# A Fourier mixing layer with a gated feed-forward on one core: fourteen instead of ten row tiles in seven products, sums formed by DMA, new buffers in the last stage

## The chip, the cores and the metric

The kernel runs on one core of a Trainium2 chip. The metric is the device time of one execution in microseconds. All engines of the core work from their own queues in order: PE (matrix products), DVE and ACT (elementwise work), POOL (elementwise work, and the issue of DMAs whose descriptors it makes itself) and SP (the issue of the other DMAs).

## The reference, cut to what matters

```python
x  = A_x                                   # 1 x 2048 x 448
xn = layernorm(x)                          # over the last axis
a  = einsum("bsd,ed->bse", xn, dft_hid_re)
b  = einsum("bsd,ed->bse", xn, dft_hid_im)
s  = einsum("ts,bse->bte", dft_seq_re, a) - einsum("ts,bse->bte", dft_seq_im, b)
g  = silu((gelu(xn @ w_gate) * (xn @ w_up)) @ w_down)     # 448 -> 1792 -> 448
out = x + s * g
```

All inputs are float32. The kernel splits operands into a high part rounded to the matmul's type and a low rest, and forms a product from two or three matmuls of the parts.

## The kernel before

There are 16 row tiles of 128 tokens (`NK`), read as four chunks of four. The work runs through these stages.

- **Normalization, and the first group of the feed-forward** (to about 73 us).
- **Blocks.** The remaining six groups `gi` = 1 to 6 of the feed-forward each take two of the 14 column tiles. `strassen` handles one column tile `f` for one half `p` of the tokens; four calls per group (`bi` = 0 to 3) make 24 blocks in a row. A block has five banks of products (x1 to x5), four pieces of the down product that are sent in between (`dn`, `send`, `down_one`), and at one place in the middle `preps()`, which prepares the weights of a later block. `prep_s` is that: four sums of 128 columns (L237 to L240; on POOL in blocks 2, 3, 5, 7 and every second one to 19, counted from 0), then two copies on ACT (L241, L242) and two subtractions on DVE (L243, L244) which split the weights. They stand on ACT and DVE between the block's own reads of its banks.
- **Hidden stage.** For each of 16 row tiles `k`, `hid_mm` makes the transforms a and b (22 matmuls); `hid_out` then either splits them plainly (`hid_plain`, six tiles `KP`) or forms eight half rows and their sums and splits seven of these (`hid_seven`, ten tiles). After the first two tiles the eight last pieces of the down product are sent.
- **Last stage.** Output rows are made in pairs `j` = 0 to 7 of two tiles each. A row tile k of the sum over the sequence goes into both outputs of a pair, either in seven products for the pair (`seven`: 7 matmuls of 448 columns and 7 of 224) or plainly (`plain`: 12 matmuls of 448). Ten tiles go in seven products and six plainly. The work is cut into units: two sevens to a loaded piece, each piece with its coefficients `ct` and two further sums of them on DVE (`combine_c`); 13 units per pair. `gather` combines the seven results into both outputs, `give` adds the plain part, multiplies by g and adds x, all on DVE; SP stores.

Four of the ten tiles (`KX`) do not fit in the core's memory together: two pairs of them take turns in two buffers, stored once to `td` and loaded again in each pair. The sums of coefficients that need no data are formed in DRAM during the blocks: `sum_copy(j)` copies by SP, `sum_add(j)` adds by two DMAs on POOL (L629), in turns, one call per block, ahead of the block's `strassen`.

The order of the work is written out by hand: the recording order of the program is each engine's order.

Of the kernel before, what the change touches and what calls it, by code (L numbers as in the profile page):

```python
# [30 lines left out]
KR = (0, 2, 4, 6, 9, 12)  # L31
KX = ((5, 8), (11, 14))
KP = (1, 3, 7, 10, 13, 15)
F_AT = {0: 0, 2: 0, 4: 1, 5: 0, 6: 1, 8: 0, 9: 1, 11: 0, 12: 1, 14: 1}

WHERE = "BAC"
UNITS = 13
DRAIN = {12: 2, 2: 2}


def order(j):


    q = [(t, k) for t in range(2) for k in KP]
    q = [q[i : i + 4] for i in range(0, 12, 4)]
    first = [KX[(j + 1) % 2], q[0]]
    return first[:: 1 if j else -1] + [KR[0:2], KR[2:4], KR[4:6], KX[j % 2], q[1], q[2]]

NS = 5


def slot_of(j, n):

    seven = [isinstance(what, tuple) for what in order(j)]
    return (0 if seven[n] else NS) + sum(s == seven[n] for s in seven[:n]), seven[n]

# [3 lines left out]
def fnet_geglu(ctx: ExitStack, tc: tile.TileContext, x, ct, et, wgu, wd, out):  # L62
# [20 lines left out]
    ps_mm = ctx.enter_context(tc.tile_pool(name="ps_mm", bufs=4, space=bass.MemoryType.PSUM))  # L83
    ps_tp = ctx.enter_context(tc.tile_pool(name="ps_tp", bufs=2, space=bass.MemoryType.PSUM))
    ps_o = ctx.enter_context(tc.tile_pool(name="ps_o", bufs=1, space=bass.MemoryType.PSUM))
# [6 lines left out]
    a_w = [sb.tile([P, 2560], FR, name=f"w{i}", tag=f"w{i}") for i in range(3)]  # L92
    a_d = [sb.tile([P, 1792], FR, name=f"wd{i}", tag=f"d{i}") for i in range(2)]
    a_r = sb.tile([P, 2 * 1536], F32, name="raw")
    a_t = sb.tile([P, 8 * 512], F32, name="tmp", tag="tmp")
# [16 lines left out]
    turns = [0]  # L112

    def o_tile(name, which=None):

        turns[0] += 1
        tag = which or "AB"[turns[0] % 2]
        return ps_o.tile([P, 512], F32, name=name, tag=tag)
# [44 lines left out]
    def turn_mm(c, k):  # L163
        pt = ps_tp.tile([P, 4, P], F32, name=f"pt{c}_{k}", tag="tp")
# [115 lines left out]
    def gu_ps(f, c):  # L280
        names = [f"gu{f}_{c}_{g}" for g in range(2)]
        if (f, c) == (0, 1):
            return [o_tile(n) for n in names]
        return [ps_mm.tile([P, 512], F32, name=n, tag="mm") for n in names]


    hs_of = {}

    def hs_tile(name, dt=FR):
        return sb.tile([P, 2, 512], dt, name=name, tag="hs", bufs=6)  # L290

    def new_hs(f, c):
        hs_of[f, c] = hs_tile(f"hs{f}_{c}")
        return hs_of[f, c]
# [3 lines left out]
    def act(f, c, pg):  # L298
        acts[0] += 1
        gt = tmp(acts[0] % 2)  # L300
# [17 lines left out]
    def down_one(gi, c, wdn, kk):  # L318
        if gi > 0 and kk >= 2:
            po = ps_tp.tile([P, 512], F32, name=f"po{gi}_{c}_{kk}", tag="tp")  # L320
        else:
            po = o_tile(f"po{gi}_{c}_{kk}")
# [36 lines left out]
    def strassen(f, p, w, late, dn, preps):  # L359
# [7 lines left out]
        def bank(i):  # L367
            return ps_mm.tile([P, 512], F32, name=f"x{i}_{f}_{p}", tag="mm")
# [19 lines left out]
        dn[1]()  # L388
        preps()
# [28 lines left out]
    with tc.manual_schedule():  # L418
# [11 lines left out]
        junk = hs_tile("junk")[:, 0]  # L430
# [124 lines left out]
        xf[2] = hs_tile("xf2", F32)  # L555
# [23 lines left out]
        for c in (2, 3):  # L579
# [6 lines left out]
            if c == 2:  # L586
                xf[3] = hs_tile("xf3", F32)
# [30 lines left out]

        sums = [dram.tile([P, NS, 512], F32, name=f"sums{j}") for j in range(NK // 2)]

        def sum_copy(j):
            src = ct[j, :NS].rearrange("n p c -> p n c")
            for q in range(2):
                nc.sync.dma_start(sums[j][:, :, 256 * q : 256 * (q + 1)], src[:, :, :256])

        def sum_add(j):
            src = ct[j, :NS].rearrange("n p c -> p n c")
            for n in (slice(0, 2), slice(2, NS)):
                nc.gpsimd.dma_start(sums[j][:, n], src[:, n, 256:768], accum_op=ALU.add)  # L629
# [13 lines left out]
        for gi in range(1, len(GROUPS)):  # L643
# [39 lines left out]
            def e_split(b):  # L683

                r = n_raw["e", b]
                if b == 3:
                    e_at[b] = []
                    for i in range(2):
                        w = a_w[slots[2 if i == 0 else 0]]
                        h, q = w[:, 1792 : 1792 + D], r[:, i * D : (i + 1) * D]  # L690
# [4 lines left out]
                if b == 1:  # L695
                    v = a_d[(gi + 1) % 2]
                else:
                    v = a_w[slots[2 if b == 0 else 0]][:, :1792]
# [3 lines left out]
            for bi, (i, p, prep) in enumerate(  # L702
# [33 lines left out]
        a_u = [sb.tile([P, 4096], FR, name=f"ts{p}", tag=f"u{p}") for p in range(2)]  # L736
# [3 lines left out]
        TS, ab = {}, {}  # L740
        fs = [a_r[:, : 4 * D], None]

        def hid_mm(k):
# [3 lines left out]
            for r in range(2):  # L747
                p = ps_mm.tile([P, 512], F32, name=f"ab{k}_{r}", tag="mm")
# [8 lines left out]
        def hid_plain(k, ps):  # L757
            spots = PLAIN[k]()
# [8 lines left out]
        def hid_seven(k, ps):  # L767


            f = fs[F_AT[k]].rearrange("p (i d) -> p i d", d=HD)  # L770
# [4 lines left out]
            nc.vector.tensor_sub(f[:, 4], f[:, 7], f[:, 0])  # L775
            nc.vector.tensor_sub(f[:, 3], f[:, 6], f[:, 7])
            nc.vector.tensor_sub(f[:, 5], f[:, 6], f[:, 4])
            nc.vector.tensor_sub(f[:, 1], f[:, 2], f[:, 5])
            t = SEVEN[k]()
            v = t.rearrange("p (i w d) -> p i w d", i=7, w=2)  # L780
            split(v[:, :, 0], v[:, :, 1], f[:, :7])
            TS[k] = t
            if k in td and k < NK - 2:
                nc.sync.dma_start(td[k], t.bitcast(F32))


        new = {}

        def place(name):

            if name not in new:
                if name[0] == "u":
                    new[name] = a_u[int(name[1])]
                elif name[0] == "x":
                    new[name] = a_x[int(name[1])]
                elif name == "t":
                    new[name] = sb.tile([P, 4096], FR, name="ts_t", tag="tmp")
                else:
                    new[name] = sb.tile([P, 8 * D], FR, name=f"ts_{name}", tag=name)
            return new[name]  # L800

        def seven_at(name):
            return lambda: place(name)[:, : 7 * D]

        def rest_of(*names):
            return lambda: [place(n)[:, 7 * D : 9 * D] for n in names]

        def in_hs(k):
            return lambda: [
                hs_tile(f"ab{k}_{r}").rearrange("p a b -> p (a b)")[:, : 2 * D] for r in range(2)  # L810
            ]

        SEVEN = dict(zip(KR, map(seven_at, ("u0", "u1", "t", "x0", "x1", "x2"))))
        SEVEN.update({k: seven_at(f"g{i}") for ks in KX for i, k in enumerate(ks)})
        spots = (rest_of("u0", "u1"), in_hs(1), in_hs(2), rest_of("t", "x0"), in_hs(3))
        PLAIN = dict(zip(KP, spots + (rest_of("x1", "x2"),)))

        def hid_out(k, ps):
            (hid_seven if k in SEVEN else hid_plain)(k, ps)


        pieces = [(j, n) for j in range(NK // 2) for n in range(8)]
        ring, bufs, c_raw = [], {}, {}

        def where(i):
            return WHERE[i % 3]

        waiting = {b: [i for i in range(len(pieces)) if where(i) == b] for b in "ABC"}

        def load_c(b):  # L830

            if waiting[b]:
                i = waiting[b].pop(0)
                j, n = pieces[i]
                c_raw[i] = bufs[b]
                s, seven = slot_of(j, n)
                if seven:
                    o = 512 if b == "B" else 0
                    nc.sync.dma_start(bufs[b][:, o : o + 768], ct[j, s][:, 256:])
                    nc.sync.dma_start(bufs[b][:, o + 768 : o + 1280], sums[j][:, s])  # L840
                else:
                    o = 768 if b == "B" else 0
                    nc.sync.dma_start(bufs[b][:, o : o + 1024], ct[j, s])

        def combine_c(i):


            v = c_raw[i].rearrange("p (i d) -> p i d", i=7)
            r, o = (2, 0) if where(i) == "B" else (0, 5)
            nc.vector.tensor_add(v[:, o], v[:, r + 4], v[:, r])  # L850
# [256 lines left out]
```

## Time and profile before

| what | value |
|---|---|
| median of 3 runs | 789.08 us (788.94 to 789.13) |
| profiled execution, its own time | 788.96 us |
| span of the profile | 787.2 us |
| PE busy | 780.8 us, 99% |
| DVE, ACT, POOL busy | 560.5, 297.9, 45.5 us |
| mean granted clock of PE | 0.999 |
| DMA moved | 123.81 MB |

The span runs from the first to the last instruction; the profiled execution's own time is 1.8 us longer. In rows of the order of time the first number is the start from the span's beginning, the second the duration, and what stands in square brackets is the idle time of the engine before the row and what ended it; "issue" means that nothing the profile shows was waited for. In rows of groups the numbers after the bar are busy time and the mean duration of one in ns, then idle time before them. In rows of DMA issues the last number is the median time from issue to landing. Names such as `sums<-ct` say what is written from what. L numbers are lines of the kernel.

### The profile page before, as it was taken

What the parts mean: (1) busy time and instruction counts of PE and PEld (TensorE: products, weight loads), DVE (VectorE), ACT (ScalarE), POOL (GpSimd) and SP (SyncE); (2) the same over time, 40 slices, a digit from 0 to 9 for tenths busy, and PEclk for the clock granted to TensorE, in tenths of its full rate; (3) what the DMA queues carried; (4) which work ended last, traced back from release to release, by engine and by line L of the source; (5) the groups of instructions that cost most, each with busy time, mean ns of one, the idle gap of its engine ahead of it and who ended that gap; (6) DMA issues with size and microseconds to landing.
All of it is one profiled execution on the core that took longest, in us unless ns stands there. A gap on an engine that the chain in (4) does not pass through costs nothing.

```text
span 787.2 us, 10474 instructions
## 1 busy us (share of the span) xinstructions
PE 780.8 (99%) x4028; PEld 701.4 (89%) x4028; DVE 560.5 (71%) x879; ACT 297.9 (38%) x482; POOL 45.5 (6%) x64
## 2 busy tenths in 40 slices
PE   9999999999999999999999999999999999999997
PEld 7888888888888888888889999999999999999997
DVE  7877777776777677676774566776858585868676
ACT  3874442322222222232231845433434344343341
POOL 1001111031021021000000000000000000000000
PEclk9999999999999999999999999999999999999999
DMA  8001465375374383110100364959595867758590
GB/s 317 25 1 54 118 161 90 94 161 90 96 164 87 103 186 57 31 43 1 47 1 1 141 237 151 393 208 351 174 344 179 309 231 274 271 210 322 193 348 30
DMA packets 46769, 123.81 MB, mean 157 GB/s; under 512 B 3840, under 2 KB 22144, under 8 KB 43776
## 3 DMA queue, kind: packets, MB, share of 16 engines
q1 hardware_dynamic: 41344, 112.67, 40.6%
q0 software_dynamic: 5376, 10.49, 8.7%
q8 instruction: 31, 0.51, 0.3%
q14 instruction: 18, 0.15, 0.1%
HBM read 109.38 MB, written 34.73 MB: 183 GB/s over the span
## 4 chain that ended last, share of the span: by engine, by line
PE 98%; DVE 1%; issue 0%; ACT 0%
PE x L347 23%; PE po L327 17%; PE p L948 15%; PE ab L753 9%; PE p L949 7%; PE x L355 6%; PE py L961 5%; PE py L963 5%; PE py L962 5%; PE gu L278 4%; PE warm L441 1%; PE pt L166 1%; PE gu L459 1%; DVE st L134 0%; DVE xr L157 0%
## 5 line engine op out<-in xcount | busy, mean ns | idle before, releaser
L327 PE MATMUL po<-wd,hs 128*128 128x448 f32 x672 | 153.0, 366 | 0.0
L327 PEld LDWEIGHTS po<-wd,hs 128*128 128x128 f32 x672 | 125.8, 188 | 14.3
L347 PE MATMUL x<-xt,w 128*128 128x512 f32 x504 | 135.0, 391 | 0.0
L347 PEld LDWEIGHTS x<-xt,w 128*128 128x128 f32 x504 | 94.7, 188 | 16.9
L336 DVE TENSOR_TENSOR gacc<-gacc,po 128x448 f32<-128x448 f32 x96 | 59.0, 618 | 57.8 <-PE po L327 57.8
L347 PE MATMUL x<-thl,w 128*128 128x512 f32 x288 | 77.4, 391 | 0.0
L753 PE MATMUL ab<-w,xt 128*128 128x448 f32 x256 | 68.0, 365 | 0.0
L347 PEld LDWEIGHTS x<-thl,w 128*128 128x128 f32 x288 | 54.1, 188 | 10.9
L355 PE MATMUL x<-xt,w 128*128 128x512 f32 x192 | 59.2, 390 | 0.0
L398 ACT ACTIVATE hs<-tmp 128x512 fp32r<-128x512 f32 x24 | 15.2, 633 | 97.2 <-DVE tmp L396 97.2
L753 PEld LDWEIGHTS ab<-w,xt 128*128 128x128 f32 x256 | 48.1, 188 | 3.8
L387 ACT ACTIVATE tmp<-x 128x512 f32<-128x512 f32 x24 | 14.3, 597 | 88.7 <-PE x L355 88.7
L355 PEld LDWEIGHTS x<-xt,w 128*128 128x128 f32 x192 | 36.1, 188 | 7.6
L887 DVE TENSOR_TENSOR w<-raw,w 128x896 fp32r<-128x896 f32 x27 | 29.4, 1091 | 12.2 <-ACT w L886 11.3
L948 PE MATMUL p<-ts_g,xt 128*128 128x448 f32 x119 | 38.0, 374 | 0.0
L887 DVE TENSOR_TENSOR xt<-raw,xt 128x896 fp32r<-128x896 f32 x25 | 27.0, 1090 | 12.0 <-ACT xt L886 11.9
L753 PE MATMUL ab<-wd,xt 128*128 128x448 f32 x96 | 35.1, 365 | 0.0
L948 PE MATMUL p<-ts_g,w 128*128 128x448 f32 x105 | 33.5, 374 | 0.0
L278 PE MATMUL gu<-xt,w 128*128 128x512 f32 (+1 forms) x154 | 31.9, 363 | 0.0
L949 PE MATMUL p<-ts_g,xt 128*128 128x224 f32 x119 | 31.5, 265 | 0.0
L881 ACT ACTIVATE w<-raw 128x640 fp32r<-128x640 f32 x27 | 19.9, 737 | 26.3 <-PE py L962 10.9
L278 PEld LDWEIGHTS gu<-xt,w 128*128 128x128 f32 x154 | 25.8, 189 | 4.4 <-DVE xt L173 0.2
(248 smaller groups left out, 1622.2 us busy)
## 6 DMA issues: line engine op xcount, KB each, us to landing
ts_g<-td SPq DMA_DIRECT2D x16, 1568.0 KB, 10.6
sums<-ct SPq DMA_DIRECT2D x16, 640.0 KB, 6.8
raw<-ct SPq DMA_DIRECT2D x26, 384.0 KB, 4.2
raw<-ct SPq DMA_DIRECT2D x17, 512.0 KB, 8.1
raw<-wgu SPq DMA_DIRECT2D x14, 512.0 KB, 3.6
raw<-sums SPq DMA_DIRECT2D x26, 256.0 KB, 4.5
td<-ts_g SPq DMA_DIRECT2D x4, 1568.0 KB, 6.1
sums<-ct POOLq DMA_DIRECT2D x8, 768.0 KB, 7.5
```

The source lines that it names most:

```text
L278: nc.tensor.matmul(ps[:, cols], a, xt[:, k, cols], start=n == 0, stop=n == len(mm) - 1)
L327: nc.tensor.matmul(po[:, :D], hs[:, a, kk * P : (kk + 1) * P], wdn[:, b, i], start=n == 0, stop=n == 5,)
L336: nc.vector.tensor_add(ga, ga, po[:, :D])
L347: nc.tensor.matmul(ps, a[i], b[j], start=first and n == 0, stop=n == 2, skip_group_check=True)
L355: nc.tensor.matmul(ps, w["k3" + "gu"[g]][0], xt[:, 3], start=False, stop=True, skip_group_check=True)
L753: nc.tensor.matmul(p[:, :D], a, b, start=n == 0, stop=n == len(mm) - 1)
L887: nc.vector.tensor_sub(lv, src, hv)
L948: nc.tensor.matmul(ps[q][:, :D], a, v, start=first, stop=False, skip_group_check=True)
L949: nc.tensor.matmul(ps[q][:, :HD], b, v[:, :HD], start=False, stop=last, skip_group_check=True)
L961: nc.tensor.matmul(py[t][:, :D], a, vh, start=first, stop=False)
L962: nc.tensor.matmul(py[t][:, :D], a, vl, start=False, stop=False)
L963: nc.tensor.matmul(py[t][:, :D], b, vh, start=False, stop=last)
```

## The change

Fourteen of the 16 row tiles now go in seven products; `KP` keeps two. With the coefficients stored in seven column blocks per tile, (r2, r2, r2, i2, r1, i2, i1), four sums are needed per tile instead of two per half piece: three are formed in DRAM by DMA and the fourth (`sum_c`, 128 columns) on DVE. `ct` holds a piece per pair and tile, `cp` the coefficients of the plain tiles. A pair has 16 units: 14 sevens and one plain unit for each output.

- **Sums in DRAM.** `sum_step(at)` replaces `sum_copy` and `sum_add`. It is called once after each of the 24 blocks, with `at` = 0 to 23, and in the hidden stage with 24 and 25. For pair j it copies three column blocks of all 14 tiles at `at` = 3j (two DMAs on SP), adds three column blocks at 3j + 2 (five accumulating DMAs on POOL, three tiles each, the last two) and adds one more column block at 3j + 4 (again five).
- **Buffers.** All memories are laid out anew: the weights are one tile `a_ws`, the feed-forward's activations `a_h` two tiles of 7 x 448, PSUM is eight named banks given in turn. `AT` says where each of the 14 split tiles lies. Tiles 0 and 1 share their buffers with 12 and 13; the stores of 0 and 1 (`keep`, 1568 KB each) go out on POOL, those of 12 and 13 on SP.
- **Hidden stage.** The split of tile k (`hid_split`) is recorded after the sums of tile k + 1 (`behind`); the outputs of tiles 14 and 15 are taken after the last matmul.
- **Last stage.** Five raw buffers (`raw_key`) are loaded ahead, four slots hold split coefficients; unit m records the sum of unit m + 4, the split of unit m + 3 and the load of the unit that follows in its raw buffer. The banks of a pair move on by one with each pair. `give` adds x by an accumulating DMA on POOL and stores the output from POOL.
- **Blocks.** In the first two blocks the places of the four down pieces change, and in block 1 `preps()` is recorded before the second place.

```diff
-KR = (0, 2, 4, 6, 9, 12)
-KX = ((5, 8), (11, 14))
-KP = (1, 3, 7, 10, 13, 15)
+KR = (2, 3, 4, 5, 6, 7, 8, 9, 11, 14)
+KX = ((12, 13), (0, 1))
+KP = (10, 15)
+KS = sorted(KR + KX[0] + KX[1])
+NS = len(KS)
...
 def order(j):
...
+    return [*KX[j % 2], *KR, *KX[(j + 1) % 2]]
...
-        dn[1]()
-        preps()
+        if f == GROUPS[1][1] and p == 0:
+            preps()
+            dn[1]()
+        else:
+            dn[1]()
+            preps()
...
-        sums = [dram.tile([P, NS, 512], F32, name=f"sums{j}") for j in range(NK // 2)]
-
-        def sum_copy(j):
-            src = ct[j, :NS].rearrange("n p c -> p n c")
-            for q in range(2):
-                nc.sync.dma_start(sums[j][:, :, 256 * q : 256 * (q + 1)], src[:, :, :256])
-
-        def sum_add(j):
-            src = ct[j, :NS].rearrange("n p c -> p n c")
-            for n in (slice(0, 2), slice(2, NS)):
-                nc.gpsimd.dma_start(sums[j][:, n], src[:, n, 256:768], accum_op=ALU.add)
+        sums = [dram.tile([P, NS, 3 * P], F32, name=f"sums{j}") for j in range(NK // 2)]
+
+        def sum_step(at):
...
+            for d in (0, 2, 4):
+                j = (at - d) // 3
+                if (at - d) % 3 or not 0 <= j < NK // 2:
+                    continue
+                src = ct[j].rearrange("k p c -> p k c")
+                if d == 0:
+                    for n in (slice(0, 7), slice(7, NS)):
+                        nc.sync.dma_start(sums[j][:, n], src[:, n, : 3 * P])
+                    continue
+                for k in range(0, NS, 3):
+                    n = slice(k, min(k + 3, NS))
+                    if d == 2:
+                        a, b = sums[j][:, n], src[:, n, 3 * P : 6 * P]
+                    else:
+                        a, b = sums[j][:, n, 2 * P :], src[:, n, 4 * P : 5 * P]
+                    nc.gpsimd.dma_start(a, b, accum_op=ALU.add)
...
-                at = 4 * gi + bi - 6
-                if 0 <= at < NK and at % 2 == 0:
-                    sum_copy(at // 2)
-                elif 0 <= at < NK:
-                    sum_add(at // 2)
                 dn = [send] * 4
                 if gi == 1 and bi < 2:
-                    dn = [[nop, nop, send, send], [send, nop, send, nop]][bi]
+                    dn = [[nop, send, nop, nop], [nop, send, send, send]][bi]
                 late = strassen(grp[i], p, ws[i], late, dn, prep)
+                sum_step(4 * gi + bi - 4)
...
+        def keep(k, eng=nc.sync):
+            eng.dma_start(td[k], TS[k].bitcast(F32))
+
+        def hid_split(k):
...
+            TS[k] = AT[k]()[:, :T7]
+            v = TS[k].rearrange("p (i w d) -> p i w d", i=7, w=2)
+            nc.scalar.activation(v[:, :, 0], f, AF.Copy)
+
+            def low():
+                nc.vector.tensor_sub(v[:, :, 1], f, v[:, :, 0])
+                if k in KX[1]:
+                    keep(k, nc.gpsimd)
...
+        def raw_key(m):
+            return m % 3 if m < 9 else (m - 11) % 5
...
+                nc.sync.dma_start(v[:, : 3 * P], ct[j, KS.index(k)][:, 4 * P :])
+                nc.sync.dma_start(v[:, 3 * P : 6 * P], sums[j][:, KS.index(k)])
+
+        def sum_c(m):
...
+                nc.vector.tensor_add(v[:, 6 * P :], v[:, 5 * P : 6 * P], v[:, 2 * P : 3 * P])
...
+            if k == 14:
+                sum_c(1)
+                prep_c(1)
+                sum_c(2)
+                behind.pop(0)()
+                keep(13)
+                ps14 = ps
+                continue
...
+        hid_plain(NK - 1, ps, [unit_at(0), unit_at(1)])
+        sums14 = hid_sums(14, ps14)
...
+            def out_():
+                nc.vector.tensor_mul(c, c, gx[t])
+
+                nc.gpsimd.dma_start(c, xv[:, 2 * j + t, :D], accum_op=ALU.add)
+                nc.gpsimd.dma_start(ov[:, 2 * j + t], c)
+                load_gx(j + 1, t)
```

The lines named in the prediction of the changed kernel: L235 to L238 are the four sums of `prep_s` on POOL (L237 to L240 before), L240 its second copy on ACT (L242 before), L643 the accumulating DMAs of `sum_step`, L843 and L846 the split of a tile in `hid_split`.

More of the change, by code (lines that the diff above doesn't have):

```diff
@@ L28, with fnet_geglu @@
 HD = D // 2
-KR = (0, 2, 4, 6, 9, 12)
-KX = ((5, 8), (11, 14))
-KP = (1, 3, 7, 10, 13, 15)
[L34 to L38, printed above, removed]
-def order(j):
[L44 to L57, printed above, removed]
+KR = (2, 3, 4, 5, 6, 7, 8, 9, 11, 14)
[3 more added lines that the diff above has]
+NS = len(KS)
+def order(j):
+    return [*KX[j % 2], *KR, *KX[(j + 1) % 2]]
 @with_exitstack
-def fnet_geglu(ctx: ExitStack, tc: tile.TileContext, x, ct, et, wgu, wd, out):
+def fnet_geglu(ctx: ExitStack, tc: tile.TileContext, x, ct, cp, et, wgu, wd, out):
     nc = tc.nc
@@ L110, in fnet_geglu, with bank, in_turn, o_tile @@
     gacc = [part(a_g[c // 2], c % 2 * 4 * D, 4, D) for c in range(NC)]
[L112 to L118, printed above, removed]
+    def bank(i, name):
+        return psum.tile([P, 512], F32, name=name, tag=f"b{i}")
+    turns = {"mm": 0, "tp": 0, "o": 0, "all": 0}
+    def in_turn(kind, name):
+        first, n = {"mm": (0, 4), "tp": (4, 2), "o": (6, 2), "all": (0, 8)}[kind]
+        turns[kind] += 1
+        return bank(first + turns[kind] % n, name)
+    def o_tile(name):
+        return in_turn("o", name)
+    def mm_tile(name):
+        return in_turn("mm", name)
+    def tp_tile(name):
+        return in_turn("tp", name)
     def split(h, l, src):
@@ L747, in hid_mm @@
             for r in range(2):
[L748 removed]
+                p = (mm_tile if k < 2 else in_turn8)(f"ab{k}_{r}")
                 mm = [(xth[c][:, b, sl], e_at[b][r]) for b in range(4)]
@@ L787, in fnet_geglu @@
[L787 to L800, printed above, removed]
@@ L815, in fnet_geglu @@
[L815 to L843, printed above, removed]
@@ new lines, in fnet_geglu, with raw_at, slot_at @@
+        units = [(j, k) for j in range(NK // 2) for k in order(j) + ["t0", "t1"]]
+        UN = NS + 2
+        def raw_key(m):
+            return m % 3 if m < 9 else (m - 11) % 5
+        def raw_at(m):
+            i = (2, 0, 1, 3, 4)[raw_key(m)]
+            return a_r[:, 896 * i :][:, :896] if i < 3 else new["d0"][:, 896 * (i - 3) :][:, :896]
+        def slot_at(m):
+            return (
+                lambda: (rest(a_x[1]), rest(a_x[2])),
+                lambda: (rest(new["tmp"]), rest(a_x[0])),
+                lambda: (unit_at(2), unit_at(3)),
+                lambda: (unit_at(4), rest(a_x[3])),
+            )[m % 4]()
@@ L898, in fnet_geglu @@
                 late[1]()
-            if k == NK - 2:
-                prep_c(0)
-                combine_c(1)
-            if k < NK - 1:
-                hid_out(k, ps)
+                sum_step(24)
+            if k == 2:
+                sum_step(25)
+            if k == NK - 1:
+                break
+            if k == 14:
[6 more added lines that the diff above has]
+                continue
+            if k in KP:
+                hid_plain(k, ps, [rest(new[u]) for u in ("u0", "u1")])
+            else:
+                hid_sums(k, ps)()
+            while behind:
+                behind.pop(0)()
+            if k not in KP and k < 14:
+                behind.append(lambda k=k: hid_split(k)())
             if k < 2:
```

387 lines of the change are left out of this document (193 added, 194 removed).

## The prediction

> **What bounds the kernel now.** I read the page's first and fourth parts, then the stretches by stage, then the order of time on PE, and last the queue of POOL, because the change gives POOL most of its new work.
>
> ```profile
> span 787.2 us, 10474 instructions
> ...
> PE 780.8 (99%) x4028; PEld 701.4 (89%) x4028; DVE 560.5 (71%) x879; ACT 297.9 (38%) x482; POOL 45.5 (6%) x64
> ...
> PE 98%; DVE 1%; issue 0%; ACT 0%
> ```
> ```profile
> 106.00:410.00 304.00, 304.00 (x1392) 260.98 (x1391) 219.62 (x330) 84.59 (x134) 37.44 (x50) 1.00 0.38 89
> 410.00:490.80 80.80, 80.80 (x400) 74.92 (x399) 45.19 (x74) 40.32 (x51) 0.00 (x0) 1.00 0.34 129
> ...
> 527.00:747.00 220.00, 220.00 (x1279) 207.63 (x1278) 160.60 (x231) 86.22 (x144) 0.00 (x0) 1.00 0.73 260
> ```
> The second fence's columns are stretch and length, then busy time of PE, PEld, DVE, ACT and POOL, the granted clock, the DMA share and GB/s. PE is never idle in the blocks (106 to 410), the hidden stage or the last stage: every matmul removed is worth its pitch, and every wait that reaches PE costs its whole length. The pitch is in the order of time on PE:
>
> ```profile
> 527.17 0.37 PE L948 MATMUL p<-ts_g,xt 128*128 128x448 f32 x1
> ...
> 531.57 0.37 PE L961 MATMUL py<-ts,w 128*128 128x448 f32 x1
> ...
> 536.44 0.36 PE L948 MATMUL p<-ts,w 128*128 128x448 f32 x1
> ```
> From the first row to the second lie 2 units of seven products, so one takes 4.40/2 = 2.20 us. To the third lie 24 plain matmuls in 4.87 us; a tile k for both outputs of a pair needs 12, so 2.435 us.
>
> **The change on PE.** Four tiles k move from plain to seven products in each of 8 pairs: 32 x (2.435 - 2.20) = 7.5 us less. Nothing else leaves the path: the hidden stage keeps 22 matmuls per tile, and blocks 0 and 1 send four groups of the down product as before.
>
> **What POOL gets.** Block n means 4(gi-1)+bi, 0 to 23. Per pair j the old sum_add put two accumulating DMAs on POOL's queue (512 and 768 KB). The new sum_step puts ten: five with rows of 384 (576 KB each, the last 384 KB), which I call A(j), and two steps later five with rows of 128 (192 KB, the last 128 KB), B(j). The rows of POOL now:
>
> ```profile
> 109.80 0.46 POOL L237 TENSOR_TENSOR raw<-raw 128x128 f32<-128x128 f32 x1 [11.87 <-DVE gacc L336]
> ...
> 157.34 1.18 POOL L629 DMA_DIRECT2D sums<-ct  x1 [30.50 <-DMA sums<-ct]
> 163.83 1.23 POOL L629 DMA_DIRECT2D sums<-ct  x1 [5.31 <-issue]
> 164.59 1.31 POOL L237 TENSOR_TENSOR raw<-raw 128x128 f32<-128x128 f32 x1
> ...
> 166.80 0.80 POOL L240 TENSOR_TENSOR raw<-raw 128x128 f32<-128x128 f32 x1
> ```
> ```profile
> POOL sums L629 <- issue: 49.7, 9, 7.4
> ```
> ```profile
> ts_g<-td SPq DMA_DIRECT2D x16, 1568.0 KB, 10.6
> sums<-ct SPq DMA_DIRECT2D x16, 640.0 KB, 6.8
> raw<-ct SPq DMA_DIRECT2D x26, 384.0 KB, 4.2
> ...
> td<-ts_g SPq DMA_DIRECT2D x4, 1568.0 KB, 6.1
> sums<-ct POOLq DMA_DIRECT2D x8, 768.0 KB, 7.5
> ...
> sums<-ct POOLq DMA_DIRECT2D x8, 512.0 KB, 6.2
> ```
> The second DMA carries no semaphore wait, yet it starts 6.49 us after the first, with 5.31 us put down to "issue". The first of that size lands in 6.2 us: POOL begins the next one 0.25 us after the one before has landed. After the last DMA of a group it is free in 0.76 us. The weight preparation's adds (L237 to L240; prep n below is that of block n = 3, 5, 7 ... 19) stand in the same queue and take 3.0 us (164.59 to 167.60).
>
> So the price of a new DMA is its landing plus 0.25. By bytes, between 6.2 (512 KB) and 7.5 us (768 KB): 576 KB is 6.8, 384 KB 5.8, 192 KB 4.85, 128 KB 4.5. The smallest are extrapolated. Their lower bound is the line with no bytes at all, 3.85; the upper is the row with as many rows in it, 7.75, since 192 KB here has the 384 rows of the 768 KB one. I take the value by bytes because the two measured shapes differ in bytes and rows by the same ratio and a row of 128 carries a quarter of the data. A(j) then holds POOL for 4 x 6.8 + 0.8 = 28.0 us and its own queue for 33.0; B(j) 20.2 and 23.9. That is 57 us of queue per pair, and a pair has three blocks.
>
> **When POOL's adds are due.**
>
> ```profile
> 196.34 1.38 PE x L347 x6
> ...
> 210.57 1.38 PE x L347 x6
> ```
> ```profile
> 203.03 1.16 ACT L242 ACTIVATE w<-raw 128x1152 fp32r<-128x1152 f32 x1
> ```
> ```profile
> 206.36 0.68 DVE L395 TENSOR_TENSOR tmp<-tmp,x 128x512 f32<-128x512 f32 x1
> ```
> ```profile
> 58.07 13.61 SPq L204 DMA_DIRECT2D raw<-wgu  x2
> ```
> Blocks 9 and 10 begin at 196.34 and 210.57: 14.23 us a block, so three are 42.7 us against POOL's 57 plus 4.5 for one and a half preps. ACT splits block 9's new weights at 203.03, after POOL's adds, and behind it on ACT and DVE, in order, stands the read of x3 (to 207.04) that frees the bank which the second product of block 10 needs at 211.26. Adds later than 203.03 + 4.2 = 207.3 stop PE; block n is due at 207.3 + 14.23(n-9).
>
> Now POOL's order, walked through. The first copy goes out behind the second load of the last row quoted (about 72) and lands in about 7 us: A(0) from 80. Prep 3 needs its raw as now: 109.8 to 112.8. B(0) 113.0 to 133.2; prep 5 to 136.2; A(1) 136.9 to 164.9; prep 7 to 167.9, due 178.8. Then two batches meet between preps: B(1) from 169.9, A(2) 193.8 to 221.8, prep 9 to 224.8, due 207.3: **17.5 us late**. All later dues move by that. B(2) to 247.0 and prep 11 to 250.0 (due 253.3); A(3) to 278.7 and prep 13 to 281.7 (due 281.7). B(3) from 283.7, A(4) 307.6 to 335.6, prep 15 to 338.6, due 310.2: **28.4 late**. B(4), prep 17 to 363.8 (due 367.1); A(5), prep 19 to 395.5 (due 395.5). Sum 46.0 us.
>
> **A second late wait on the same queue.** keep(0) and keep(1), two stores of 1568 KB, now go out on POOL, behind A(7) and B(7), and the splits of tiles 12 and 13 write the buffers they read. B(5), A(6), B(6), A(7) from 397.5: 397.5 + 2 x 23.9 + 2 x 33.0 = 511.3; keep(0) ends at 517.4, in time. About 3 us after it begins, B(7): 514.3 + 23.9 = 538.2; keep(1) ends at 544.3 by the 6.1 us row.
>
> ```profile
> 428.39 62.42 PE ab L753 x308
> ```
> The hidden stage ends now at 490.81, then at 536.8; the fifth product of the first unit needs tile 14's bank at 4 x 0.314 later, 538.1. ACT's copies of tile 14 stand behind the split of tile 13 (1.52 us) and three copies of 0.54 us, 544.3 + 3.1 = 547.4: **9.3 us**.
>
> ```profile
> L887 DVE TENSOR_TENSOR w<-raw,w 128x896 fp32r<-128x896 f32 x27 | 29.4, 1091 | 12.2 <-ACT w L886 11.3 <-PE py L962 0.8
> ...
> L851 DVE TENSOR_TENSOR raw<-raw 128x256 f32<-128x256 f32 x26 | 11.1, 426 | 0.9
> ...
> L985 DVE TENSOR_TENSOR cc<-cc,gx 128x448 f32<-128x448 f32 x15 | 9.3, 622 | 0.3
> ...
> L122 DVE TENSOR_TENSOR ts_g<-raw,ts_g 128x1568 fp32r<-128x1568 f32 x3 | 5.4, 1793 | 4.9 <-ACT ts_g L121 4.9
> ...
> L121 ACT ACTIVATE ts_g<-raw 128x1568 fp32r<-128x1568 f32 x3 | 4.5, 1516 | 3.7 <-DVE raw L778 2.5 <-issue 1.2
> ...
> L771 ACT ACTIVATE raw<-ab 128x448 f32<-128x448 f32 x5 | 2.7, 540 | 9.5 <-PE ab L753 9.5
> ...
> L775 DVE TENSOR_TENSOR raw<-raw 128x224 f32<-128x224 f32 x5 | 2.0, 391 | 3.4 <-ACT raw L771 3.4
> ```
> **After a stop, PE's speed.**
>
> ```profile
> 1.49 6.26 PE warm L441 x14
> ...
> 198.93 2.74 PE x L347 x12
> ```
> The first 14 matmuls of 512 take 6.26 us, where later ones take 0.228 each: 3.1 us lost. I charge that once for each of three stops, 9.3 us; the bound is 0, as no row shows PE idle in the middle. The Trainium skill (TensorE: Matmul & The Clock Gate, Part 1) says that about 3.4 us of idling halve the clock until as long a busy stretch is over; that is an estimated 1.7 us a stop, and the sum would be 4 us lower.
>
> **What costs nothing, and its cover.** Four more tiles are split in seven: DVE 4 x 0.39 + 1.79 = 3.4 and ACT 2.6 us under a tile's 4.46 us of PE. DVE's 14 sums of 128 per pair take between half of 0.426 and all of it, about 4.2 us; with 14 x 1.09, two plain splits and 13 steps of 0.62 it is 29 us of the pair's 35.7. Without that cover each unit would slip by what is over. With five raw buffers a unit's load goes out some 2.1 us into the unit four before the one in which its sum is made, 4 x 2.2 - 2.1 = 6.7 us, and PE wants it some 4 us later; the 384 KB row says 4.2, and a td load ahead of it on SP's queue (10.6 us to land) is what could make it late. The pair moves 10.6 MB instead of 9.4: at the 356 GB/s that 260 at a share of 0.73 gives, 29.8 us of 35.7. SP's issues rise from 21 to 34 per pair, off the path. POOL's add of x and store of the output (bound 7.5 + 6.1 us) have nine units, 19.8 us. At the end c0 is finished after c1, so DVE runs about 0.9 us past PE; I add that.
>
> **Sum**, against the profiled execution's own 788.96 us (median 789.08): 788.96 - 7.5 + 46.0 + 9.3 + 9.3 + 0.9 = **847 us**.
>
> **Rivals.** (1) *POOL keeps up.* If the wait before the next DMA is far shorter than its landing, or small rows land faster, the blocks are untouched and 788.96 - 7.5 + 0.9 gives 782.4. In the same walk with one interval for all DMAs there is no late prep at 4.5 us, and 7.2 us late at 4.7: below about 4.7 this rival decides. For it: nothing of POOL's wait for a landing has a semaphore, so its cause is unseen. Against it: these unnamed waits came to 49.7 us in 9 places. The Trainium skill (DMA: Bandwidth & Descriptors, Anatomy of one DMA) fits such a DMA with 2.0 us plus its bytes at 436 GB/s, which is an estimated 3.4 us for 576 KB and 2.5 for 192 KB, and this rival would follow. By that rule 512 KB would take 3.2 us, and the trace has 6.2 for an accumulating one between two places in DRAM.
> (2) *POOL keeps up, but the last stage starves.* If DMAs move no more than the present 260 GB/s, a pair takes 10.6 MB/260 = 40.8 us instead of 35.7: 8 x 5.1 - 6.6 gives 823. Against it: the share is 0.73, not 1.
> (3) *Longer small DMAs.* With 7.75 us for 192 KB the walk gives 114 + 50 us of stops, 955; halfway (7.3 and 6.3) 93 + 35, 920. With 6.45 for 576 KB and 3.85 for 192 KB it gives 21 and none, 803.
> (4) *No change on balance*, a small lateness that eats the 7.5 us.
>
> **How the numbers follow.** Lateness as forecast 0.78, of which 0.06 above 900; rival 1 0.13; rival 2 0.07; rival 4 0.02. The range is 800 to 900: it leaves out 0.13 below and 0.06 above. The three chances, with 0.2% (1.6 us) as what a measurement tells from no change: faster 0.13, same 0.02, slower 0.85.
>
> **What would show it.** POOL's timeline with DMAs of L643 each 4.5 to 7 us behind the one before; ACT's split of weights (L240) waiting for POOL in blocks 9 and 15, nearly not in 5, 7, 11 and 17; PE idle in two stretches of some 18 and 28 us near 207 and 290 and one after the hidden stage, behind ACT L843; units at 2.20 us. DMAs of POOL one to two us apart, no PE idle and about 782 us would prove me wrong; so would PE idle spread over the units of the last stage.

## The result and the profile after

The changed kernel takes 887.24 us (median of 4 runs, 886.23 to 890.07) against 789.01 us beside it: a ratio of 1.125, 95% interval 1.122 to 1.128. The forecast was 847 us, range 800 to 900. The sign and the mechanism of the stops in PE's work were right; the sum was 40 us short, and the loss in the last stage had no term in it. The profiled execution took 886.23 us, with a span of 884.5.

First the page of after: its head, busy times, the clock in 40 slices, the chain, and POOL's group; then the waits.

```profile
span 884.5 us, 11136 instructions
...
PE 787.1 (89%) x4092; PEld 702.1 (79%) x4092; DVE 562.0 (64%) x933; ACT 309.2 (35%) x430; POOL 141.7 (16%) x158
...
PEclk9999999998599995799999999879999999999999
...
issue 50%; PE 18%; POOL 13%; DMA 13%; DVE 5%; ACT 1%; SPq 1%; POOLq 0%; DVEq 0%; ACTq 0%
...
L643 POOL DMA_DIRECT2D sums<-ct x80 | 97.6, 1220 | 371.6 <-issue 369.1
...
sums<-ct SPq DMA_DIRECT2D x16, 1344.0 KB, 10.8
sums<-ct POOLq DMA_DIRECT2D x32, 576.0 KB, 6.3
```
```profile
POOL sums L643 <- issue: 369.1, 79, 10.7
...
ACT w L240 <- POOL raw L238: 85.1, 6, 35.0
...
PE x L346 <- DVE tmp L398: 62.6, 4, 30.6
...
ACT ts_u L843 <- DMA td<-ts_u: 16.9, 1, 16.9
...
PE p L979 <- ACT f L822: 16.6, 1, 16.6
```

PE fell from 99% busy to 89%. The chain that was 98% PE is now half "issue", for the most part the unnamed wait of POOL between two accumulating DMAs, which comes to 369 us in 79 places over the whole run. The waits lead from there to PE: ACT's weight split (L240) waits for POOL's adds (L238), PE for the DVE work behind that split. The stretches by stage show when, in the columns told in the prediction:

```profile
73.00:212.50 139.50, 138.34 (x630) 117.85 (x628) 95.95 (x148) 42.03 (x69) 34.26 (x37) 1.00 0.71 162
212.50:242.40 29.90, 0.09 (x2) 0.04 (x1) 2.62 (x4) 1.16 (x1) 7.86 (x9) 0.55 0.56 86
242.40:246.00 3.60, 3.60 (x9) 3.11 (x10) 3.27 (x6) 1.58 (x3) 0.00 (x0) 0.50 0.79 188
...
331.40:362.00 30.60, 0.00 (x0) 0.00 (x0) 2.56 (x3) 1.16 (x1) 7.85 (x9) 0.56 0.59 88
362.00:365.50 3.50, 3.45 (x9) 2.95 (x10) 3.15 (x6) 1.39 (x3) 0.00 (x0) 0.50 0.85 181
...
562.00:579.00 17.00, 0.45 (x1) 0.46 (x2) 2.86 (x3) 3.42 (x6) 1.74 (x2) 0.64 0.54 172
579.00:584.00 5.00, 5.00 (x19) 4.61 (x19) 3.80 (x8) 3.20 (x4) 0.00 (x0) 0.51 0.95 359
584.00:880.00 296.00, 286.00 (x1735) 268.08 (x1734) 204.82 (x338) 116.75 (x133) 20.36 (x28) 0.99 0.83 279
```

Two stops of PE in the blocks (29.8 us at 212.5, 30.7 at 331.4) and one of 16.6 after the hidden stage, each with some 3.5 to 5 us at a granted clock of half behind it. Between the stops the blocks ran at full clock with a DMA share of 0.64 to 0.71, as a mean over the stretch. From PE's order of time, by stage:

| stage | before, us | after, us | difference |
|---|---|---|---|
| blocks (first product to first ab) | 336.5 | 406.5 | +70.0 |
| hidden stage | 81.2 | 81.2 | 0 |
| last stage (to PE's end) | 292.4 | 315.6 | +23.2 |
| PE's end to the end of the span | 4.15 | 8.36 | +4.2 |

### The profile page after: what moved, and what is told of

Its sections match the earlier page's. It is cut to its first block, busy times and chain, and to the rows that moved or that the text cites. A ratio compares the mean times of both kernels' runs of the same rounds, so it can differ in the third digit from the quotient of the medians.

```text
span 884.5 us, 11136 instructions
## 1 busy us (share of the span) xinstructions
PE 787.1 (89%) x4092; PEld 702.1 (79%) x4092; DVE 562.0 (64%) x933; ACT 309.2 (35%) x430; POOL 141.7 (16%) x158
## 4 chain that ended last, share of the span: by engine, by line
issue 50%; PE 18%; POOL 13%; DMA 13%; DVE 5%; ACT 1%; SPq 1%; POOLq 0%; DVEq 0%; ACTq 0%
POOL sums L643 10%; DMA cc<-x 6%; PE p L979 5%; PE gu L276 3%; PE po L326 2%; PE p L980 2%; DMA raw<-sums 2%; PE x L346 2%; DMA raw<-wgu 1%; DMA ts_u<-td 1%; DMA f<-sums 1%; DVE xt L120 1%; DMA td<-ts_u 1%; DMA out<-cc 1%; PE pt L164 1%
## 5 line engine op out<-in xcount | busy, mean ns | idle before, releaser
L643 POOL DMA_DIRECT2D sums<-ct x80 | 97.6, 1220 | 371.6 <-issue 369.1
L326 PE MATMUL po<-wd,hs 128*128 128x448 f32 x672 | 155.7, 370 | 0.1
L242 DVE TENSOR_TENSOR w<-raw,w 128x1152 fp32r<-128x1152 f32 x12 | 16.3, 1358 | 85.9 <-ACT w L240 85.8
L119 ACT ACTIVATE w<-raw 128x896 fp32r<-128x896 f32 (+1 forms) x42 | 37.2, 885 | 76.8 <-DVE raw L890 46.6
L980 PE MATMUL p<-ts_u,xt 128*128 128x224 f32 x224 | 61.2, 273 | 0.0
L979 PE MATMUL p<-ts_u,xt 128*128 128x448 f32 x112 | 38.9, 391 | 20.4 <-ACT f L822 16.6
L979 PE MATMUL p<-xt,w 128*128 128x448 f32 x168 | 53.6, 375 | 0.0
L980 PEld LDWEIGHTS p<-ts_u,xt 128*128 128x128 f32 x224 | 44.8, 200 | 0.5 <-DVE xt L120 0.3
L240 ACT ACTIVATE w<-raw 128x1152 fp32r<-128x1152 f32 x12 | 13.9, 1162 | 86.5 <-POOL raw L238 85.1
L890 DVE TENSOR_TENSOR raw<-raw 128x128 f32<-128x128 f32 x71 | 20.4, 287 | 37.1 <-DMA raw<-sums 36.6
```

The lines of the kernel that those rows point to most:

```text
L119: nc.scalar.activation(h, src, AF.Copy)
L242: nc.vector.tensor_sub(w[:, 1408:], raw[:, 384:], w[:, 256:1408].bitcast(F32))
L326: nc.tensor.matmul(po[:, :D], hs[:, a, kk * P : (kk + 1) * P], wdn[:, b, i], start=n == 0, stop=n == 5,)
L643: nc.gpsimd.dma_start(a, b, accum_op=ALU.add)
L890: nc.vector.tensor_add(v[:, 6 * P :], v[:, 5 * P : 6 * P], v[:, 2 * P : 3 * P])
L979: nc.tensor.matmul(ps[q][:, :D], hn, v, start=first, stop=False, skip_group_check=True)
```

## The experiments

My theory was POOL's queue: the accumulating DMAs hold POOL, and what stands behind them (weight adds, two stores) comes late. Open were the cause of the unnamed wait, the 14 us of stops beyond the forecast, and the last stage, which lost time although its units run at 2.19 us. Runs e1, e4, e5 and e6 are one execution each; only differences of nearly 10 us and more are read from their times.

**Is it the accumulating DMAs?** e1 leaves them out.

```diff
-                for k in range(0, NS, 3):
+                for k in range(0, 0, 3):
```


> This run leaves out all accumulating DMAs of the coefficient sums (the 80 of L643), so the last stage multiplies with unfinished sums; every other instruction stays. Theory (POOL's queue is the cause of the stops): without them the weight preparation's adds and the two stores on POOL are on time, the stops of 29.8, 30.7 and 16.6 us and the half-clock stretches behind them go, and 887.2 - 77.1 - 6 gives about 804; if the small waits of the last stage and the later end came from the same queue too, down to 789 - 7.5 = 782. Rival (SP's copies of 1344 KB, the bytes of all DMAs, or the new buffers hold PE): PE still idles 20 us or more in the blocks and the time stays above 830.

Measured 800.4 us. No wait of L240 for POOL is left, and no stop is longer than 2.8 us. The DMAs of POOL cost 87 us. The theory's first figure holds (804), not its second (782): some 12 us over the kernel before stay, which these DMAs have no part in.

**What is the unnamed wait?** e2 doubles the memory for POOL's descriptors; e6 leaves it and cuts the DMAs to a third of their rows.

```diff
-    nc = bacc.Bacc("TRN2", target_bir_lowering=False, num_devices=1, dynamic_dma_scratch_size=1024)
+    nc = bacc.Bacc("TRN2", target_bir_lowering=False, num_devices=1, dynamic_dma_scratch_size=2048)
```


> Only the size of the memory kept for POOL's own DMA descriptors changes, from 1024 to 2048 per partition. Theory A (the unnamed wait between two accumulating DMAs is one for free descriptor memory): the second DMA of a batch begins about 1.2 us after the first, the mean distance of two falls below 4.7 us, POOL keeps up, and the time comes to 790 to 805. Theory B (each accumulating DMA waits for the landing of the one before, whatever the memory): distances stay at 6.4 and 4.6 us and the time at 887.

```diff
-                for k in range(0, NS, 3):
-                    n = slice(k, min(k + 3, NS))
+                for k in range(NS):
+                    n = slice(k, k + 1)
```


> The descriptor memory stays at 1024 per partition; each accumulating DMA takes one tile (128 rows) instead of three, 28 per pair instead of ten. Theory A (POOL waits for free descriptor memory; a DMA of a third of the rows takes a third of it, so the next can be issued while the one before runs): distances of 1.2 to 2.5 us, 34 to 60 us per pair, POOL keeps up or is late by a few us, 795 to 830. Theory B (POOL waits for the landing of the one before): 28 distances of 4 to 4.8 us, over 112 us per pair, and the time is above 1050.

e2 took 801.3 us (ratio 1.016, 1.014 to 1.017), e6 806.2. POOL's timeline for the first batch A(0), in after, e2 and e6:

```profile
79.85 1.46 POOL L643 DMA_DIRECT2D sums<-ct  x1 [2.56 <-DMA sums<-ct]
87.82 1.23 POOL L643 DMA_DIRECT2D sums<-ct  x1 [6.52 <-issue]
94.28 1.22 POOL L643 DMA_DIRECT2D sums<-ct  x1 [5.24 <-issue]
100.72 1.23 POOL L643 DMA_DIRECT2D sums<-ct  x1 [5.21 <-issue]
107.12 1.14 POOL L643 DMA_DIRECT2D sums<-ct  x1 [5.18 <-issue]
```
```profile
80.64 2.71 POOL L643 DMA_DIRECT2D sums<-ct  x2 [2.88 <-DMA sums<-ct]
87.94 1.23 POOL L643 DMA_DIRECT2D sums<-ct  x1 [4.59 <-issue]
92.15 1.22 POOL L643 DMA_DIRECT2D sums<-ct  x1 [2.99 <-issue]
97.10 1.13 POOL L643 DMA_DIRECT2D sums<-ct  x1 [3.72 <-issue]
```
```profile
79.32 2.70 POOL L643 DMA_DIRECT2D sums<-ct  x3 [2.53 <-DMA sums<-ct]
84.76 0.83 POOL L643 DMA_DIRECT2D sums<-ct  x1 [2.74 <-issue]
```
With twice the memory two go out back to back (one row, x2, 2.71 us) before the wait begins; with a third of the rows, three do. The second then starts long before the first can have landed (6.3 us in after), and in e2 the third, at 87.94, starts 0.3 us after the first has landed. So POOL doesn't wait for the landing of the DMA before as such but for descriptor memory, which comes free with a landing: in the smaller memory one DMA of 384 rows or three of 128 find room, in the doubled one two of 384. In e2 the "issue" waits of L643 come to 161 us instead of 369, and no stop is left in the blocks but one of 1.2 us.

**What costs is what stands behind them.** e3 keeps the DMAs, moves the adds to DVE (three places like the first one here) and the stores to SP; e4 moves the stores alone.

```diff
-                    nws[0] = prep_s(slots[2], n_raw[0], nc.gpsimd)
+                    nws[0] = prep_s(slots[2], n_raw[0], nc.vector)
...
-                    keep(k, nc.gpsimd)
+                    keep(k)
```


> The weight preparation's adds go on DVE instead of POOL, and the stores of tiles 0 and 1 on SP instead of POOL. All 80 accumulating DMAs stay. Theory (what costs is work that stands behind them in POOL's queue): POOL is as late as before but nobody waits for it, the three stops go, 10 preps cost DVE some 4 x 0.35 us each under blocks of 14.2 us, and the time is 787 to 805. Rival (the DMAs themselves slow SP's loads or the weights' loads): stops in the blocks remain, and the time is 830 or more.

> Only the stores of tiles 0 and 1 move from POOL to SP. Theory: the stop of 16.6 us after the hidden stage and the half clock behind it go, those in the blocks stay: 887.2 - 16.6 - 2.7 = 868. Rival (tile 13's split waits for something else than POOL's queue, as the landing of the store itself or DMA load): the stop stays, 880 to 890.

e3 took 852.9 us (1.079, 1.076 to 1.083), where 787 to 805 was expected. As expected, no stop over 3.3 us is left in the blocks or after the hidden stage; but POOL, still late, met a third user that I had left out of the expectation.

```profile
ACT cc L999 <- DMA out<-cc: 39.8, 1, 39.8
...
PE py L991 <- ACT cc L999: 38.2, 1, 38.2
```
```profile
604.97 1.13 POOL L643 DMA_DIRECT2D sums<-ct  x1 [3.35 <-issue]
605.68 1.36 POOL L1016 DMA_DIRECT2D cc<-x  x1
```
The last DMA of the sums goes out at 604.97, when the second pair of the last stage should long be over, and the first addition of x (L1016) right behind it. Until its output is stored, `cc` isn't free for the next gather, and the bank that ACT should read isn't free for PE: a stop of 38.2 us at 575.7. Moving work away from a queue that can't keep up moved the stop to the next user.

e4 took 877.5, where 868 was expected. The stop of 16.6 us is gone, but waits of 3.0, 1.7 and 2.8 us in the first pair stand in its place: the pair came to 46.4 us from 58.9, and not to 35.6. The two stops in the blocks stayed, at 62.3 us.

**Why were the stops longer than forecast?** e5 leaves out three quarters of SP's copies. Of its edit, in part:

```diff
-                    for n in (slice(0, 7), slice(7, NS)):
+                    for n in (slice(0, 7), slice(7, NS)) if j < 2 else ():
```


> The sums of all pairs are added, by the same 80 accumulating DMAs, into the two tiles of pairs 0 and 1 in turn, so SP copies only for these two pairs (4 copies of 1344 KB instead of 16); the last stage reads coefficients of the same size in the place of the sums, so its results are left out. Theory (the copies by SP run beside the accumulating DMAs and lengthen them, which is why the stops in the blocks came to 60.5 us and not the 46.0 of the prediction): the one or two distances of 8 to 12 us in a batch shrink to 6.5 (576 KB) and 4.7 us (192 KB), the stops in the blocks come to 40 to 50 us, and the time to 868 to 878. Rival (the long distances come from the weights' loads or from the accumulating DMAs themselves): stops stay at 58 us or more, 883 to 890.

It took 852.6 us, where 868 to 878 was expected: stops of 18.4 and 22.7 us in the blocks and 7.1 after the hidden stage, where the forecast of before had 17.5, 28.4 and 9.3. (The expectation left the last out, so its time was too high.) POOL's rows of A(1) in after, the copies that run beside them, and A(1) in e5:

```profile
141.98 1.27 POOL L643 DMA_DIRECT2D sums<-ct  x1 [0.44 <-issue]
150.42 1.24 POOL L643 DMA_DIRECT2D sums<-ct  x1 [7.17 <-issue]
161.15 1.23 POOL L643 DMA_DIRECT2D sums<-ct  x1 [9.50 <-issue]
168.83 1.23 POOL L643 DMA_DIRECT2D sums<-ct  x1 [6.45 <-issue]
```
```profile
150.62 1.27 SPq L635 DMA_DIRECT2D sums<-ct  x2
```
```profile
142.03 1.27 POOL L643 DMA_DIRECT2D sums<-ct  x1 [0.46 <-issue]
148.56 1.24 POOL L643 DMA_DIRECT2D sums<-ct  x1 [5.27 <-issue]
155.19 1.23 POOL L643 DMA_DIRECT2D sums<-ct  x1 [5.39 <-issue]
161.87 1.23 POOL L643 DMA_DIRECT2D sums<-ct  x1 [5.45 <-issue]
```
The fourth DMA begins 26.9 us after the first with the copies beside it, 19.8 without. The distances alone are 6.5 to 6.7 us, near the 6.8 priced; the price left out what the copies by SP add. While they run, from 150.4 to 165 us, the DMA engines are full: the share is 0.97 and then 1.06, against 0.72 in e5 from 148.6 to 168.5. The profile of before already had this, but the prediction took the medians. The old DMAs (before, L629), from issue to landing:

```profile
DMA to landing us min/median/max: 6.0/6.8/11.5
```
Three of the eight of 768 KB, each with a copy of SP under way beside it, landed in 10.7 to 11.5 us; the other five took 7.4 to 7.6.

**The last stage.** Lengths of the eight pairs, from the starts of PE's units (a pair without a wait is 35.57 us; before it was 36.5):

```
pair     0      1      2      3      4      5      6      7
after  58.85  35.59  35.87  36.42  36.08  38.57  36.74  37.45
e2     43.71  35.59  35.57  36.79  37.45  36.60  36.37  36.94
e7     44.11  35.75  37.09  37.02  37.02  37.15  36.69  37.06
e8     44.71  35.57  35.57  36.41  37.15  37.09  37.75  36.51
e13    45.15  35.56  35.59  36.54  36.47  36.87  37.23  37.71
e11    41.63  35.57  36.09  36.41  36.63  36.70  36.52  36.81
e10    41.39  35.56  35.79  37.25  37.35  38.57  37.44  37.52
e14    41.23  35.59  35.57  35.57  35.57  35.57  35.57  35.73
```
All runs but after have the larger descriptor memory. e7 gives the first pair two more raw buffers, e11 loads these earlier. Of e7, in part; e11 records the last two lines earlier, in the hidden stage:

```diff
-            return m % 3 if m < 9 else (m - 11) % 5
+            return (0, 1, 2, 0, 1, 5, 6, 2, 0, 3, 4)[m] if m < 11 else (1, 2, 0, 3, 4)[(m - 11) % 5]
...
+            if raw_key(m) > 4:
+                return cc[:, 896 * (raw_key(m) - 5) :][:, :896]
...
-        LOAD_AT = (6, 8), (2, 6)
+        LOAD_AT = (3, 5), (2, 6)
...
+        load_c(5)
+        load_c(6)
```


> With descriptor memory of 2048. In the first pair of the last stage two more raw buffers (in the memory of the output's rows, free until the first gather) take the coefficients of units 5 and 6, and the loads of tiles 0 and 1 from DRAM are recorded at units 3 and 5 instead of 6 and 8. Theory (the first pair loses 8 us because three raw buffers give a load no more than 6.6 us, and the two loads of tiles go out late): the first pair goes from 43.7 to 36 to 37 us and the time from 801.3 to 793 to 795. Rival (the bandwidth of the loads at the start of the stage holds it): the first pair stays at 41 us or more, 799 to 802.

> As the run before with two more raw buffers in the first pair, but their loads are recorded ahead of those of units 7 and 8 on SP, so that they go out at the end of the hidden stage (about 492.6) and not at 499.3. Theory (the first pair loses its 8 us to loads that go out too late, first those of units 3 and 4 through three buffers, then the two tiles): the stop of 5.3 us in unit 4 goes, the first pair comes to 36 to 38 us and the time to 793 to 796. Rival (bandwidth at the start of the stage holds the loads): the first pair stays at 41 us or more, 799 to 802.

e7 took 801.5 us. Units 7 and 12, at 4.2 and 4.7 us in e2, fell to 2.19, but one wait of 5.3 us came in at unit 4: on SP the load of unit 5 stood behind that of unit 8, and went out only at 499.3. e11, with it ahead, took 798.2 (1.012, 1.010 to 1.014): that wait is 1.0, and one of 2.1 us at unit 12 is left. The first pair is short of loads in time, and I got back 2 of its 8 us. Its 44.1 us in e7 and 41.6 in e11 are on the rival's side of 41: in e11 the DMA share is 0.95 to 1.02 from 486 to 517 us, so the engines are full there, where in e2 it was 0.67 to 0.79 from 502 to 517. How much of what is left is bandwidth and how much is order isn't shown.

e8 and e13 change DVE's order at the end of a pair, so that the bank which the next pair's first unit needs is read earlier (L1056 ahead of one split in e8; of one split, with the other ahead of the gather, in e13).

Of e13, in part:

```diff
             if u == NS - 1:
+                prep_c(m + 3)
                 todo = gather(ps)
                 for f in todo[:3]:
                     f()
-                prep_c(m + 3)
             elif u == NS:
                 for f in todo[3:]:
                     f()
+                c = cs[0][0]
+                nc.vector.tensor_add(c, c, py[:, :D])
                 prep_c(m + 3)
-                c = cs[0][0]
-                todo = [lambda c=c, py=py: nc.vector.tensor_add(c, c, py[:, :D])]
```


> With descriptor memory of 2048. DVE's addition of the first output's plain product (L1056), which frees the bank that the first unit of the next pair needs for its seventh product, is recorded ahead of the split of a unit's coefficients instead of behind it, 1.1 us of DVE work earlier. Theory (that bank holds the first unit of pairs 3 to 7): these units go from 2.9 to 3.5 us to 2.2 to 2.4, and the time from 801.3 to 795 to 797. Rival (these units wait for coefficients that load late): they stay above 2.8 us, 799 to 802.

> With descriptor memory of 2048. On DVE, around the end of a pair: the split for the next pair's first unit is recorded ahead of the gather, and L1056 right behind the gather, ahead of the split for the second unit; the order alone changes. Theory (first units of 2.9 to 3.5 us are DVE's order: the bank is read too late): first units and those behind them at 2.2 us, pairs 3 to 7 at 35.6 to 36, and the time 795 to 797. Rival (DVE is short of time in these units, or loads are late): the loss only moves to other units, pairs 36.4 us or more, 800 to 802.

They took 801.9 and 802.9 us. The first unit of pair 3 fell from 3.39 to 2.19 in both, but in e13 the second rose to 2.66 and the tenth to 2.70: the rival, the loss only moved. e10 puts all of this together, with the order of the first two blocks as before and the end's last operations partly on POOL. With the new buffers that order probably changes what the first two blocks compute, which isn't shown; only the last stage of this run is read.

> All together: descriptor memory of 2048, both edits of the last stage, the first two blocks' order of before (down pieces and weight preparation), and at the end the first output's last three operations on POOL beside DVE's. Theory: 801.3 less 7 (first pair), 5 (first units), 1.2 (the gap at 85) and 1.5 (end) is 786 to 788, below the 788.9 of the kernel before. Rival (losses move instead of going): 790 to 796.

It took 800.5 us, with pairs of 37.3 to 38.6 from the fourth on: not better than e11 alone. The last run takes away the loads of split tiles in pairs 1 to 7.

```diff
-                    nc.sync.dma_start(TS[n].bitcast(F32), td[n])
+                    if j == 0:
+                        nc.sync.dma_start(TS[n].bitcast(F32), td[n])
```


> As the run before it of 798.2 us (descriptor memory of 2048, two more raw buffers in the first pair), but the loads of the split tiles from DRAM (two of 1568 KB per pair) are left out in pairs 1 to 7, so these pairs multiply with old tiles; first pair as it was. Theory (the coefficient loads of the plain units and of the next pair's first units queue behind the load of a tile, so that ACT, DVE and with them the gather start late and the next pair's first unit waits for its bank): first units of pairs 2 to 7 go from 2.7 to 3.3 us to 2.2, pairs to 35.6, and the time to 791 to 794. Rival (DVE has too much to do at the end of a pair, whatever the loads): first units stay at 2.7 us or more, 796 to 800.

It took 789.8 us (1.001, 1.000 to 1.002), and every pair from the second on is clean. The end of pair 3 in e11 (SP, ACT, DVE) and in e14 (SP, ACT):

```profile
623.91 0.38 SPq L1042 DMA_DIRECT2D ts_u<-td  x1
625.21 1.57 SPq L883 DMA_DIRECT2D raw<-cp  x2
```
```profile
634.73 1.29 ACT L119 ACTIVATE w<-raw 128x512 fp32r<-128x512 f32 x2 [5.25 <-DMA raw<-cp]
```
```profile
637.61 0.61 DVE L1006 TENSOR_TENSOR cc<-cc,p 128x448 f32<-128x448 f32 x1
...
643.87 0.61 DVE L1061 TENSOR_TENSOR cc<-cc,py 128x448 f32<-128x448 f32 x1
```
```profile
620.15 2.52 SPq L883 DMA_DIRECT2D raw<-cp  x2
```
```profile
629.01 0.63 ACT L119 ACTIVATE w<-raw 128x512 fp32r<-128x512 f32 x1 [1.24 <-PE p L984]
```
In e11 the coefficients of the plain units go out behind 1568 KB of a tile, ACT waits 5.25 us for them, DVE begins the gather late (637.61) and reads the bank at 643.87 (L1061 there, L1056 in after), when the next pair's first unit has begun at 641.7. In e14 ACT waits for PE, no longer for a load. DVE's order in e8 and e13 only chose which unit paid.

e14 takes away the bytes of the td loads together with their place in SP's queue, so it doesn't tell which of the two costs the time. In e11, from 613.4 to 634 us, while the two loads of pair 3 are in flight, the DMA share is 0.97 and then 1.05: the engines have no room left. POOL's addition of x stands in another queue, and it too landed late, in 9.6 us against 6.2 in e14 (medians after the first pair).

No version tried is faster than the kernel before.

## Why the prediction was right, and where it was short

- **PE's saving, 7.5 us: right.** Units take 2.19 to 2.20 us; a clean pair 35.57 instead of 36.5, about 7.6 us over eight.
- **POOL's wait and its prices: right in size.** 6.4 to 6.7 us where 6.8 was priced and no copy runs beside, 4.6 where 4.85; rival 3 falls with that. Its cause was unseen in before; e2 and e6 show descriptor memory. That decides rival 1: POOL keeps up as soon as the memory is doubled, but the time is then 801 and not 782. The Trainium skill (DMA: Bandwidth & Descriptors, Anatomy of one DMA) gives an estimated 3.4 us for 576 KB; the trace has 6.3 for its landing, and the measurement decides.
- **The late adds, 46.0 us: the mechanism right, the size short.** Blocks 9 and 15 as forecast (at 212.5 and 331.4 us; the walk's own dues were 207.3 and 310.2), with 29.8 + 30.7 = 60.5 us instead of 17.5 + 28.4. The term that was mis-sized is the price of a DMA: it took the medians of before, 6.2 and 7.5 us, and lacked SP's copies, which lengthen the distances beside them to between 7.7 and 11.9 us. Without three quarters of them the two stops are 41.1 (e5).
- **The late store, 9.3 us: the same mis-sizing.** 16.6 us, behind ACT L843 as forecast: keep(1) went out at 567.6 and not 538. e5 has 7.1.
- **The clock, 9.3 us: near in sum, by luck.** Half clock for 3.6, 3.5 and some 5 us behind the three stops (rows above) and 3.4 behind a fourth of 2.0 us at 608.7; half of each is lost, 8 us in all. That is 1.7 to 2.5 us a stop where 3.1 was charged, for four stops instead of three. The Trainium skill (TensorE: Matmul & The Clock Gate, Part 1) agrees with each of the first two: its estimate was 1.7 us a stop, the rows give 1.8. Before the fourth, 2.0 us of idling were enough, less than the 3.4 named there; the measurement decides.
- **"What costs nothing, and its cover": the step that failed.** It said that a load has 6.7 us and needs 4.2, and named a td load ahead of it as what could make it late; I put no price on that. It costs 8 us in e2's first pair and 6.3 in pairs 2 to 7 (in after 7.7), and e14 shows the second part to be the td loads. Rival 2 had the bandwidth of a whole pair as its cause, at 260 GB/s; the pairs move 279 at a mean share of 0.83, so as a mean it doesn't bind. But for 20 us of each pair, while the td loads run, the engines are full. Whether order in SP's queue or these full 20 us cost the time stays open.
- **The end, 0.9 us: 4.2.** The gather now begins with only the two plain units, 4.9 us of PE, ahead; before it had twice as much. DVE's chain from it, in after:

```profile
871.34 0.62 DVE L1001 TENSOR_TENSOR cc<-cc,p 128x448 f32<-128x448 f32 x1
...
881.08 0.39 DVE L1071 TENSOR_TENSOR cc<-cc,f 128x224 f32<-128x224 f32 x1
```
  That is 10.1 us, while PE ends at 876.1. I had counted which output is finished last, and not the start of the gather.
- **Blocks otherwise.** Small waits of PE come to 3.3 us in the blocks; one of 1.2 us at 85 is in e1 and e2 too, where the order of block 1 is new, and gone in e10, which has the old order. It had no place in the sum.

Sum by what was measured: 789.0 - 7.6 + 60.5 + 16.6 + 8.0 + 4.2 + 3.3 + 7.7 is 881.7; some 2 us more lie in the first pair, and about 3 aren't assigned.

## What to carry to other kernels

A queue is judged by all its users: before work is added to one, list everything that stands behind it to the end of the kernel, since relief of one user only hands the lateness to the next (e3). A wait without a semaphore between two DMAs of the same engine can be a wait for descriptor memory; doubling that memory, or smaller DMAs, tells in one run. And a hidden load's price is read with what is ahead of it in its queue and with what else the DMA engines carry just then: means of 0.7 and 0.83 hid stretches at a share of about 1, in which single DMAs took 1.5 to 2 times as long as without.

## What was not expected

The size of one memory moved the time by 86 us: 887.2 to 801.3. Copies issued by SP lengthened the distance of accumulating DMAs in another queue from 6.5 to as much as 11.9 us (at 390.4), though the mean share of the DMA engines in the first blocks was 0.71. And cutting the same bytes into 112 + 112 DMAs instead of 80 made the kernel 81 us faster (e6), though each of the 224 holds POOL for a mean of 0.88 us, against 1.22 for one of the 80.
